# Chunks of 448 and 512 tokens, and tiles placed at chosen distances mod 256 bytes, in a spectral mixer with a squared-ReLU MLP

## The chip, the cores and the metric

The kernel runs on one core of a Trainium2 chip, in fp32 data with fp32r products. The metric is the device time of one execution in microseconds. The time before is 2588.85 us, the median of three runs (2587.41 to 2589.65).

## The reference

Eight sequences of 3008 tokens and 256 features go through a real FFT along the tokens, a complex 256 x 256 product with bias, a soft threshold and the inverse FFT, and then through an MLP of width 2048 whose activation is the square of a ReLU:

```python
X = np.fft.rfft(x, axis=1)
Yr = Xr @ w_r - Xi @ w_i + b_r
Yi = Xr @ w_i + Xi @ w_r + b_i
Yr = np.sign(Yr) * np.maximum(np.abs(Yr) - lam, 0.0)      # Yi alike
y = np.fft.irfft(Yr + 1j * Yi, n=3008, axis=1)
h = np.maximum(y @ w_in, 0.0)                             # 24064 tokens, 256 -> 2048
out = h * h @ w_out                                       # 2048 -> 256
```

## The kernel before

**Stages.** The transform of length 3008 is split as 47 x 64. For each sequence there are four kinds of small products: `psa` (length 47 forward, L867 and in the start phase L460), `psb` (length 64 forward, L320), `psm` (the complex 256 x 256 product, through `mix`), `psc` (length 64 back) and `psd` (length 47 back, L368). Their result lands, five columns of the 64 at a time ("units" of 235 tokens), in the tiles `xt0` and `xt1`: a high part and a low part of the MLP's input.

**The MLP** runs over chunks of tokens (`WIDTHS`, six per sequence: 470, four of 508, 506) and, within a chunk, over eight steps `j` of 256 hidden features. One pass (`j` of a chunk) is a round; there are 48 chunks and 384 rounds. A round has:

- `mm1`: twelve matmuls into `ph`, moving operand `xt` (one column per token of the chunk), stationary operand `wi`;
- `squares` (ACT, L1060 and L1061) into `g`, seven slots of half a chunk each; `sums` (DVE, L1069 to L1071) makes three of the seven slots by subtraction;
- a round later the split of `g` into `gh` (ACT, L1114) and `gl` (DVE, L1123);
- two rounds later `mm2`: twenty-one matmuls into `po`, moving operand `gh` or `gl` (one slot, half a chunk wide), stationary operand `wo`. The seven slots are the seven products of a Strassen step over (half of the tokens, half of the features), put together by `put_together` at the chunk's end.

Each product is made of three fp32r matmuls, high x high, high x low and low x high, by the helper `mm3` (L283; its three matmuls are L286, L287 and L288, whatever the product). Each matmul loads its 128 x 128 stationary operand anew.

**Order.** The main loop is written by hand (`manual_schedule`): `plan_a`, `plan_b` and `plan_d` put the steps of the next sequence's transform at places of a round (`load`, `a1`, `p1`, `v1`, `p2`, `a2`, `v2`), so `psm`, `psc`, `psa`, `psb` and `psd` stand between the `ph` and the `po` of a round or behind the `po`. `pieces` tells which chunks a unit lies in; a unit that lies across a border is written in two pieces. The start phase (about the first 122 us: the first sequence's transform and the splitting of the weights) has an order made by a small planner, `Queue`.

**Where tiles lie.** SBUF tiles are placed one behind the other in the order in which they are allocated, so each size moves all that follow. A distance below is the start of the stationary operand minus the start of the moving one, mod 256 bytes, as the tiles' sizes and this order give it:

| product | columns | moving operand starts at | stationary at | distance |
|---|---|---|---|---|
| `ph` | 470 to 508 | `xt` 112 to 224 | `wi` 96 | 128 to 240, in steps of 16 |
| `po` | 236, 254 | `gh`, `gl`: each slot 1016 bytes behind the last | `wo` 96 | 64 to 208, in steps of 8 |
| `psm`, main loop | 256 | `wm` 224 | `xh`, `xl` 160 | 192 |
| `psm`, start phase (L545, L550) | 512 | `wm` 224 | `xh`, `xl` 224 | 0 |
| `psc`, main loop | 512 | `zh` 32, `zl` 160 | `tMs` 128 | 96, 224 |

Of the kernel before, what the change touches and what calls it, by code (L numbers as in the profile page):

```python
# [28 lines left out]
F32 = mybir.dt.float32  # L29
F32R = mybir.dt.float32r  # L30
# [4 lines left out]
P = 128  # L35
S = 3008
N1 = 47
N2 = 64
NR = 24
# [5 lines left out]
W = 5  # L45
GROUPS = [(g, min(W, N2 - g)) for g in range(0, N2, W)]

NU1 = 96
# [11 lines left out]

WIDTHS = (2 * W * N1, 508, 508, 508, 508, 506)
NCH = len(WIDTHS)

# [182 lines left out]
def fft_mix_moe(ctx: ExitStack, tc: tile.TileContext, xp, xu, w_r, w_i, b_r, b_i,  # L246
# [7 lines left out]

    NCOL = max(WIDTHS)
    HALF = (NCOL // 2 + 1) // 2 * 2

# [5 lines left out]
    def ctile(name, shape, dt=F32):  # L263
        return const.tile(shape, dt, name=name, tag=name)

    tQ = ctile("tQ", [P, 64])
    tB = ctile("tB", [P, NR + 1, N2])
    tMs = ctile("tMs", [P, 2, P], F32R)
    tD = ctile("tD", [120, 4, 120])
    sg = ctile("sg", [P, 2, NR])  # L270
    neg = ctile("neg", [P, 1])
    nc.vector.memset(neg, -LAM)
# [63 lines left out]

    nch = NCH * B
    cols = [WIDTHS[c % NCH] for c in range(nch)]
    col0 = [sum(cols[:c]) for c in range(nch)]
    assert sum(WIDTHS) == S  # L340

# [36 lines left out]
    def start():  # L378

        with ExitStack() as own:  # L380
# [4 lines left out]
            def tl(tag, shape=(P, 512), dt=F32, bufs=1, name=None):  # L385
                return sb.tile(list(shape), dt, tag=tag, name=name or tag, bufs=bufs)
# [8 lines left out]
            tM = tl("tM", (P, P))  # L395
            tU = tl("tU", (NU1, 4 * NR))
            rows = tl("rows", (33, 2 * D), F32R)
# [64 lines left out]

            a_first, a_second, a0_done = [], [], []
            for i in range(nq):
                s = {}
# [310 lines left out]

            queue.run()
            return xt, later

# [8 lines left out]
    def tl(tag, shape=(P, 512), dt=F32, bufs=1, name=None):  # L788
        return sb.tile(list(shape), dt, tag=tag, name=name or tag, bufs=bufs)
# [4 lines left out]
    def opnd(name, dt):  # L794
        return tl(name, (P, NPR, HALF), dt, bufs=2)


# [88 lines left out]
    def plan_b(b, r0):  # L886
        for i in range(NPAIR):
            def steps(i=i):
# [16 lines left out]
                def high():  # L905
                    s["h"] = tl("xh", (P, 3, 2, P), F32R)
                    nc.scalar.copy(s["h"], s["x"])

                def low():
                    s["l"] = tl("xl", (P, 3, 2, P), F32R)  # L910
                    nc.vector.tensor_sub(s["l"], s["x"], s["h"].bitcast(F32))  # L911
# [64 lines left out]
    def plan_d(b, i, r, tag):  # L976
# [10 lines left out]
        def take():  # L987
            s["v"] = tl("xh", (P, 3, 2, P), name="dv").rearrange("p a b m -> p (a b m)")
            s["v"] = s["v"][:, :2 * NR * W].rearrange("p (k m) -> p k m", k=2)
            nc.scalar.copy(s["v"][:, :, :s["ps"].shape[3]], s["ps"][:, :, 1])  # L990

        def unfolded():
            if len(parts) == 1:
                x = tl("xl", (P, 3, 2, P), name="dx").rearrange("p a b m -> p (a b m)")
            else:
                x = tl("o0", (P, 2, HALF), name="dx").rearrange("p a m -> p (a m)")
            s["x"] = x[:, :2 * N1 * W].rearrange("p (k m) -> p k m", k=2)
            unfold(i, s["ps"], s["v"], s["x"])
# [74 lines left out]
    def mm2(c, j, po, gg):  # L1073
        m, _ = halves(cols[c])
        for s, bank, half in PLACES:

            mm3(po[bank][:, half * m:half * m + m], (wo_[0][j][:, s], wo_[1][j][:, s]),
                (gg[0][:, SLOT[s], :m], gg[1][:, SLOT[s], :m]), j == 0 and half == 0, j == NU - 1,
                skip_group_check=True)

    def put_together(c, po):
        n = cols[c]
        m, t0 = halves(n)
        p = {s: po[bank][:, half * m:half * m + m] for s, bank, half in PLACES}
        o = [tl(f"o{k}", (P, 2, HALF))[:, :, :m] for k in range(2)]
# [91 lines left out]
```

## Time and profile before

| | |
|---|---|
| time, median of three runs | 2588.85 us |
| span of the profiled execution | 2588.1 us |
| TensorE (PE) busy | 2562.5 us, 99% of the span |
| weight loads (PEld) busy | 2276.4 us, 88% |
| VectorE (DVE) busy | 2104.4 us, 81% |
| ScalarE (ACT) busy | 1990.3 us, 77% |
| mean granted TensorE clock | 0.997 |

The profiled execution's span runs from its first to its last instruction and lies 0.75 us below the median of the timed runs. In a timeline a row's first number is its start and the second its length; matmuls are pipelined, so a record's end lies behind the next one's start, and the distance of two starts is what a matmul costs.

### The profile page before, as it was taken

The page shows a single profiled execution, that of the slowest core. Times are in us where ns is not written, and L with a number is a line of the kernel's source. Part 1 is how long each engine was busy: PE and PEld are TensorE (multiplying, and loading weights), DVE is VectorE, ACT ScalarE, POOL GpSimd, SP SyncE. Part 2 cuts the span into 40 slices and gives each one's busy share as a digit, 9 for nine tenths or more (in the row PEclk, how much of TensorE's full clock was granted, in tenths as well). Part 3 has the DMA queues.
Part 4 walks back from the last instruction along what each step waited for, and adds up shares of the span by engine and source line. Part 5 has one row for each costly group of instructions (what it writes and reads, how often), then busy time and mean ns, then how long its engine had stood idle before and what let it go on. Part 6 is the DMA issues. An engine that isn't in the chain of part 4 may idle for free.

```text
span 2588.1 us, 43011 instructions
## 1 busy us (share of the span) xinstructions
PE 2562.5 (99%) x16674; PEld 2276.4 (88%) x16674; DVE 2104.4 (81%) x3441; ACT 1990.3 (77%) x3048; POOL 0.2 (0%) x4
## 2 busy tenths in 40 slices
PE   7999999999999999999999999999999999999999
PEld 4599988999889998899988999899998999999998
DVE  6888887888878888788887888788887888877777
ACT  4787886787777787788877878778886788787776
POOL 0000000000000000000000000000000000000000
PEclk8999999999999999999999999999999999999999
DMA  7711114111231112311132111321114111101000
GB/s 239 226 58 41 45 55 138 46 46 48 69 121 33 49 41 90 100 40 41 47 114 79 36 41 51 123 61 36 57 42 128 49 47 55 32 25 35 17 31 17
DMA packets 125362, 171.36 MB, mean 66 GB/s; under 512 B 13157, under 2 KB 88751, under 8 KB 125159
## 3 DMA queue, kind: packets, MB, share of 16 engines
q1 hardware_dynamic: 123851, 166.73, 20.7%
q8 instruction: 133, 2.18, 0.3%
q10 hardware_dynamic: 1308, 1.87, 0.2%
q14 instruction: 70, 0.57, 0.1%
HBM read 93.50 MB, written 74.97 MB: 65 GB/s over the span
## 4 chain that ended last, share of the span: by engine, by line
PE 96%; DVE 1%; DMA 1%; ACT 1%; SPq 0%; issue 0%; ACTq 0%; DVEq 0%
PE ph L286 13%; PE ph L288 13%; PE ph L287 13%; PE po L286 12%; PE po L287 12%; PE po L288 12%; PE psd L368 3%; PE psb L320 3%; PE psm L288 2%; PE psm L287 2%; PE psm L286 2%; PE psa L867 2%; PE psa L460 1%; PE psc L287 1%; PE psc L286 1%; PE psc L288 1%
## 5 line engine op out<-in xcount | busy, mean ns | idle before, releaser
L1114 ACT CAST gh<-g 128x762 fp32r<-128x762 f32 (+3 forms) x768 | 682.5, 927 | 325.0 <-PE po L288 284.6
L1123 DVE TENSOR_TENSOR gl<-g,gh 128x762 fp32r<-128x762 f32 (+3 forms) x768 | 805.6, 1070 | 107.5 <-ACT gh L1114 106.5
L286 PE MATMUL po<-gh,wo 128*128 128x254 f32 (+1 forms) x2688 | 765.1, 285 | 0.0
L287 PE MATMUL po<-gl,wo 128*128 128x254 f32 (+1 forms) x2688 | 753.3, 280 | 0.4 <-DVE gl L1123 0.4
L288 PE MATMUL po<-gh,wo 128*128 128x254 f32 (+1 forms) x2688 | 752.6, 280 | 0.0
L286 PE MATMUL ph<-xt,wi 128*128 128x508 f32 (+2 forms) x1536 | 608.7, 396 | 4.7 <-ACT g L1060 3.2
L288 PE MATMUL ph<-xt,wi 128*128 128x508 f32 (+2 forms) x1536 | 597.3, 389 | 0.0
L287 PE MATMUL ph<-xt,wi 128*128 128x508 f32 (+2 forms) x1536 | 596.2, 388 | 0.0
L286 PEld LDWEIGHTS po<-gh,wo 128*128 128x128 f32 x2688 | 509.6, 190 | 35.8 <-issue 29.2
L1060 ACT ACTIVATE g<-ph 128x508 f32<-128x508 f32 (+1 forms) x768 | 410.8, 587 | 153.2 <-PE ph L288 150.1
L287 PEld LDWEIGHTS po<-gl,wo 128*128 128x128 f32 x2688 | 509.5, 190 | 6.9 <-DVE gl L1123 0.6
L288 PEld LDWEIGHTS po<-gh,wo 128*128 128x128 f32 x2688 | 509.6, 190 | 0.0
L1069 DVE TENSOR_TENSOR g<-g 128x508 f32<-128x508 f32 (+1 forms) x384 | 261.4, 681 | 275.1 <-ACT g L1061 275.1
L1061 ACT ACTIVATE g<-g 128x1016 f32<-128x1016 f32 (+1 forms) x384 | 401.3, 1045 | 12.2
L288 PEld LDWEIGHTS ph<-xt,wi 128*128 128x128 f32 x1536 | 288.7, 188 | 62.3
L286 PEld LDWEIGHTS ph<-xt,wi 128*128 128x128 f32 x1536 | 289.5, 188 | 60.2 <-issue 9.7
L287 PEld LDWEIGHTS ph<-xt,wi 128*128 128x128 f32 x1536 | 289.3, 188 | 45.2
L1070 DVE TENSOR_TENSOR g<-g 128x254 f32<-128x254 f32 (+1 forms) x384 | 161.7, 421 | 13.2
L1071 DVE TENSOR_TENSOR g<-g 128x254 f32<-128x254 f32 (+1 forms) x384 | 161.5, 421 | 13.2
L288 PE MATMUL psm<-wm,xl 128*128 128x256 f32 x504 | 140.2, 278 | 0.3 <-DVE xl L911 0.3
L287 PE MATMUL psm<-wm,xh 128*128 128x256 f32 x504 | 140.2, 278 | 0.0
L286 PE MATMUL psm<-wm,xh 128*128 128x256 f32 x504 | 140.1, 278 | 0.0
(106 smaller groups left out, 2463.8 us busy)
## 6 DMA issues: line engine op xcount, KB each, us to landing
bin<-s SPq DMA_DIRECT2D x96, 256.0 KB
s<-evc SPq DMA_DIRECT2D x96, 256.0 KB
xin<-in_xp_dram SPq DMA_DIRECT2D x48, 512.0 KB
din<-s SPq DMA_DIRECT2D x94, 240.0 KB
s<-eva SPq DMA_DIRECT2D x208, 96.0 KB
outT_dram<-o SPq DMA_DIRECT2D x143, 127.0 KB
w<-in_moe_w_in_dram SPq DMA_DIRECT2D x8, 512.0 KB
w<-in_moe_w_out_dram SPq DMA_DIRECT2D x8, 512.0 KB
```

The lines of the kernel that those rows point to most:

```text
L286: nc.tensor.matmul(out, l0, r0, start=start, stop=False, **kw)
L287: nc.tensor.matmul(out, l0, r1, start=False, stop=False, **kw)
L288: nc.tensor.matmul(out, l1, r0, start=False, stop=stop, **kw)
L320: nc.tensor.matmul(ps[:, k, :, q, :], tv[:, q, k], tB[:, 0:r + 2:r + 1], start=True, stop=True)
L368: nc.tensor.matmul(ps[:, k, part], t[:n, s:s + P], tD[:n, tab + part, :n], start=True, stop=True)
L1060: nc.scalar.activation(g[:, a:b + 1:b - a, :m], ph[:, :, t * t0:t * t0 + m], AF.Relu)
L1061: nc.scalar.activation(g[:, LATER - 1:, :m], g[:, LATER - 1:, :m], AF.Square)
L1069: nc.vector.tensor_sub(g[:, :2, :m], at[1][:, None].broadcast_to([P, 2, m]), ends)
L1070: nc.vector.tensor_sub(at[6], at[3], at[4])
L1071: nc.vector.tensor_sub(at[1], at[6], at[2])
L1114: nc.scalar.copy(gg[k][0][:, part, :m], hid[k][:, part, :m])
L1123: nc.vector.tensor_sub(gg[k][1][:, part, :m], hid[k][:, part, :m], gg[k][0][:, part, :m].bitcast(F32))
```

## The change

1. The chunk widths become 470, four of 512 and 490 in the first sequence and 448 and five of 512 in the other seven (`FIRST`, `OTHER`).
2. `HALF`, the room of a half chunk in `g`, `gh`, `gl` and the output tiles, is 256 columns (before 254), so slots are 1024 bytes apart; the two halves of a PSUM bank in `po` are 256 columns apart whatever the chunk's width.
3. Tiles are placed anew: some are swapped or made larger, two unused ones (`pad0`, `pad1`) are put in between, and `xh` and `xl` of the main loop lie 64 bytes into a larger tile (`shifted`).

The distances become:

| product | columns | moving operand starts at | stationary at | distance |
|---|---|---|---|---|
| `ph` | 448 to 512 | `xt` 0 | `wi` 0 | 0 |
| `po` | 224 to 256 | `gh`, `gl` 0, each slot | `wo` 64 | 64 |
| `psm`, main loop | 256 | `wm` 0 | `xh`, `xl` 64 | 64 |
| `psm`, start phase | 512 | `wm` 0 | `xh`, `xl` 0 | 0 |
| `psc`, main loop | 512 | `zh`, `zl` 0 | `tMs` 0 | 0 |

```diff
-WIDTHS = (2 * W * N1, 508, 508, 508, 508, 506)
-NCH = len(WIDTHS)
+LINE = 16
+FIRST = (2 * W * N1, 512, 512, 512, 512, 490)
+OTHER = (448, 512, 512, 512, 512, 512)
+NCH = len(OTHER)
...
-    NCOL = max(WIDTHS)
-    HALF = (NCOL // 2 + 1) // 2 * 2
+    NCOL = max(FIRST + OTHER)
+    HALF = NCOL // 2
...
+    tD = ctile("tD", [120, 4, 120])
     tMs = ctile("tMs", [P, 2, P], F32R)
-    tD = ctile("tD", [120, 4, 120])
...
-    neg = ctile("neg", [P, 1])
+    neg = ctile("neg", [P, LINE])[:, :1]
...
-    cols = [WIDTHS[c % NCH] for c in range(nch)]
+    cols = [*FIRST] + [*OTHER] * (B - 1)
...
-            tU = tl("tU", (NU1, 4 * NR))
+            tU = tl("tU", (NU1, P))[:, :4 * NR]
...
+            ctile("pad0", [P, LINE])
...
+            ctile("pad1", [P, 3 * LINE])
...
+    def shifted(tag, dt=F32, name=None):
+        t = tl(tag, (P, 6 * P + 4 * LINE), dt, name=name)
+        return t[:, LINE:LINE + 6 * P].rearrange("p (a b m) -> p a b m", a=3, b=2)
...
-                    s["h"] = tl("xh", (P, 3, 2, P), F32R)
+                    s["h"] = shifted("xh", F32R)
...
-                    s["l"] = tl("xl", (P, 3, 2, P), F32R)
+                    s["l"] = shifted("xl", F32R)
...
-            mm3(po[bank][:, half * m:half * m + m], (wo_[0][j][:, s], wo_[1][j][:, s]),
+            mm3(po[bank][:, half * HALF:half * HALF + m], (wo_[0][j][:, s], wo_[1][j][:, s]),
...
-        p = {s: po[bank][:, half * m:half * m + m] for s, bank, half in PLACES}
+        p = {s: po[bank][:, half * HALF:half * HALF + m] for s, bank, half in PLACES}
```

On TensorE the order of the kinds of products stays as it was in every one of the 384 rounds. This is the first round of the second sequence's first chunk, from the last `ph` to the first `po` (which still belongs to the chunk before). In the kernel before:

```order
L286 MATMUL ph<-xt_4288,wi_276 128x470
L287 MATMUL ph<-xt_4289,wi_276 128x470
L288 MATMUL ph<-xt_4288,wi_277 128x470
L867 MATMUL psa<-xin,tQ 64x512 x4
L286 MATMUL po_4051<-gh,wo_1092 128x254
L287 MATMUL po_4051<-gl,wo_1092 128x254
L288 MATMUL po_4051<-gh,wo_1093 128x254
```

And in the changed one, whose last chunk of the first sequence has halves of 246 columns:

```order
L288 MATMUL ph<-xt_4290,wi_277 128x448
L289 MATMUL ph<-xt_4291,wi_277 128x448
L290 MATMUL ph<-xt_4290,wi_278 128x448
L875 MATMUL psa<-xin,tQ 64x512 x4
L288 MATMUL po_4053<-gh,wo_1094 128x246
L289 MATMUL po_4053<-gl,wo_1094 128x246
L290 MATMUL po_4053<-gh,wo_1095 128x246
```

The rows stand in the same places; the widths are others, and lines lie two further down.

On ACT the pieces of units change with the borders. Here is the second unit of the second sequence, written into `xt` from `dx`, before:

```order
L990 COPY dv<-psd 128x240
L1114 CAST gh<-g 128x762
L1114 CAST gh<-g 128x1016
L1003 CAST xt_4288<-dx 128x2x235
L1060 ACTIVATE g<-ph 128x508
```

In the changed kernel the border at 448 tokens cuts this unit into 213 and 22:

```order
L998 COPY dv<-psd 128x240
L1122 CAST gh<-g 128x3x246
L1122 CAST gh<-g 128x4x246
L1011 CAST xt_4290<-dx 128x2x213
L1068 ACTIVATE g<-ph 128x2x246 x2
L1069 ACTIVATE g<-g 128x4x246
L880 COPY eva<-psa 128x512
L1122 CAST gh<-g 128x3x246
L1122 CAST gh<-g 128x4x246
L1011 CAST xt_4420<-dx 128x2x22
```

One cast more stands there, a round later, and its subtraction on DVE likewise; this comes in seven of the eight sequences.

## Rows read from the trace of the kernel before

**Rows 1.** The page: span, busy time of the engines, chain that ended last.
```profile
span 2588.1 us, 43011 instructions
PE 2562.5 (99%) x16674; PEld 2276.4 (88%) x16674; DVE 2104.4 (81%) x3441; ACT 1990.3 (77%) x3048; POOL 0.2 (0%) x4
PE 96%; DVE 1%; DMA 1%; ACT 1%; SPq 0%; issue 0%; ACTq 0%; DVEq 0%
```

**Rows 2.** Waits of PE: who for whom, us in total, times, longest.
```profile
PE psb L320 <- DMA bin<-s: 7.5, 1, 7.5
PE psa L460 <- DMA x<-in_xu_dram: 4.0, 1, 4.0
PE ph L286 <- ACT g L1060: 3.2, 2, 1.7
...
PE po L287 <- DVE gl L1123: 0.4, 1, 0.4
```

**Rows 3.** Busy time of each engine in two stretches: 470-token chunk, 508-token chunk.
```profile
core 0: us, PE busy (x) PEld busy (x) DVE busy (x) ACT busy (x) POOL busy (x), PEclk, DMA share, GB/s
449.60:499.20 49.60, 49.60 (x348) 46.58 (x347) 41.59 (x72) 39.43 (x62) 0.00 (x0) 1.00 0.12 37
499.20:551.50 52.30, 52.30 (x352) 48.04 (x351) 44.85 (x73) 41.01 (x64) 0.00 (x0) 1.00 0.14 45
```

**Rows 4.** Timeline of PE, one round: start us, length us, line, instruction.
```profile
539.38 0.40 PE L286 MATMUL ph<-xt,wi 128*128 128x508 f32 x1
...
542.14 0.28 PE L286 MATMUL psm<-wm,xh 128*128 128x256 f32 x1
...
544.27 0.28 PE L286 MATMUL po<-gh,wo 128*128 128x254 f32 x1
...
546.75 0.39 PE L286 MATMUL ph<-xt,wi 128*128 128x508 f32 x1
```

**Rows 5.** Timeline of PE, one round of a 470-token chunk.
```profile
468.40 0.38 PE L286 MATMUL ph<-xt,wi 128*128 128x470 f32 x1
...
470.96 1.05 PE L368 MATMUL psd<-tD,din 120*128 120x120 f32 x8
471.77 0.36 PE L286 MATMUL po<-gh,wo 128*128 128x236 f32 x1
471.96 0.27 PE L287 MATMUL po<-gl,wo 128*128 128x236 f32 x1
...
474.20 0.28 PE L320 MATMUL psb<-tB,bin 128*128 128x128 f32 x1
```

**Rows 6.** Timeline of PE: the psm group of an earlier round.
```profile
501.59 0.28 PE L286 MATMUL psm<-wm,xh 128*128 128x256 f32 x1
...
503.63 0.28 PE L286 MATMUL po<-gh,wo 128*128 128x254 f32 x1
```

**Rows 7.** Groups by line: psm from 501.5, psm from 542.1; whole span.
```profile
L286 PE MATMUL psm<-wm,xh 128*128 128x256 f32 x6 | 1.7, 276 | 0.0
...
L286 PE MATMUL psm<-wm,xh 128*128 128x256 f32 x6 | 1.7, 280 | 0.0
...
L287 PE MATMUL psm<-wm,xh 128*128 128x256 f32 x504 | 140.2, 278 | 0.0
L287 PE MATMUL po<-gl,wo 128*128 128x254 f32 x2240 | 630.2, 281 | 0.4 <-DVE gl L1123 0.4
```

**Rows 8.** Timeline of PE in the start phase: psm at distance 0, 512 columns.
```profile
72.14 2.11 PE L545 MATMUL psm<-wm,xh 128*128 128x512 f32 x8
74.09 1.08 PE L550 MATMUL psm<-wm,xl 128*128 128x512 f32 x4
75.00 0.59 PE L575 MATMUL psc<-zh,tM 128*128 128x512 f32 x1
```

More of the change, by code (lines that the diff above doesn't have):

```diff
@@ L337, in fft_mix_moe @@
     nch = NCH * B
-    cols = [WIDTHS[c % NCH] for c in range(nch)]
+    cols = [*FIRST] + [*OTHER] * (B - 1)
     col0 = [sum(cols[:c]) for c in range(nch)]
-    assert sum(WIDTHS) == S
+    assert sum(FIRST) == sum(OTHER) == S
     def pieces(b, i):
@@ L987, in take @@
         def take():
-            s["v"] = tl("xh", (P, 3, 2, P), name="dv").rearrange("p a b m -> p (a b m)")
+            s["v"] = shifted("xh", name="dv").rearrange("p a b m -> p (a b m)")
             s["v"] = s["v"][:, :2 * NR * W].rearrange("p (k m) -> p k m", k=2)
@@ L993, in unfolded @@
             if len(parts) == 1:
-                x = tl("xl", (P, 3, 2, P), name="dx").rearrange("p a b m -> p (a b m)")
+                x = shifted("xl", name="dx").rearrange("p a b m -> p (a b m)")
             else:
```

## The prediction

> **What bounds the kernel now.** I read the page first: its busy shares, then the chain that ended last. TensorE is busy 99% of the span, and the chain is 96% PE [rows 1]. The waits of TensorE confirm it: the longest are single events of the start, 7.5 and 4.0 us, and inside the main loop the two that name ACT and DVE are worth 3.2 and 0.4 us in all [rows 2]. So in the main loop the end is set by the sum of distances between the starts of successive matmuls, which I call their pace, and by nothing else. The other engines have room: in two stretches of one chunk each DVE is busy 41.6 us of 49.6 and 44.9 us of 52.3, ACT less [rows 3].
>
> A pace is read from the timeline, not from the "mean ns" of a group: matmuls overlap, and a record lasts about 160 ns longer than its pace. One round of 508-token work shows it: twelve ph matmuls start at 539.38 and the next kind at 542.14, so 2.76 / 12 = 0.230 us each; eighteen psm of 256 columns take 544.27 - 542.14 = 2.13 us, 0.1183 each; twenty-one po of 254 columns take 546.75 - 544.27 = 2.48 us, 0.1181 each [rows 4]. A narrow round gives 470 columns in (470.96 - 468.40) / 12 = 0.2133 and 236 columns in (474.20 - 471.96) / 20 = 0.112 [rows 5]. Between the widths one column costs (0.230 - 0.2133) / 38 = 0.00044 us in ph and (0.1181 - 0.112) / 18 = 0.00034 us in po.
>
> **What the pace depends on.** The same psm group, same shapes and same addresses, takes 2.04 us for eighteen in another round (503.63 - 501.59), 0.1133 each [rows 6]. So there are two beats, 0.1133 and 0.1183, and a group keeps the beat that it began with: the mean record is 276 ns in the one group and 280 ns in the other on the lines of all its matmuls, and 278 over all 504 of a line [rows 6, 7], so about half the groups run in each. TensorE does not stream at a rate fixed by columns alone. The trace holds one kind of product whose two operands lie at a distance of 0 mod 256 in 512 columns: psm of the start phase (wm and xh at 224 both). Of one group the first eight take 74.09 - 72.14 = 1.95 us, some 0.10 of it, by my estimate, the switch from the kind before (in a narrow round the first po after another kind costs 471.96 - 471.77 = 0.19 against 0.112 [rows 5]), so (1.95 - 0.10) / 8 = 0.231 each; the last four take 75.00 - 74.09 = 0.91, 0.2275 each [rows 8]. It began slow and ended fast, where ph at distances of 128 to 240 stays at 0.230 for 508 columns, 0.2317 at 512.
>
> The Trainium skill says otherwise: on "SBUF — State Buffer", section "SBUF: two separate sides", PE, ACT and the dedicated ports of DVE never wait on anyone, and TensorE is given two independent read ports there. By it no address distance could matter, and the sum below would keep only its width terms. The two beats of one instruction form speak against it here, whatever their cause.
>
> **The change, part by part.** Nothing is removed and no matmul is added: 4608 ph and 8064 po matmuls before and after, in the same order of kinds in each of the 384 rounds.
>
> *Widths at unchanged paces.* Before, ph is 3072 of 508, 768 of 506 and 768 of 470: 3072 x 0.230 + 768 x 0.2291 + 768 x 0.2133 = 1046.3 us. After, it is 39 chunks of 512 (3744), 672 of 448, 96 each of 490 and 470: 3744 x 0.2317 + 672 x 0.2036 + 96 x (0.2221 + 0.2133) = 1046.1. po before: 6720 x 0.1181 + 1344 x 0.112 = 944.2. After: 6552 of 256 at 0.1188, 1176 of 224, 168 each of 246 and 236. Nothing here shows a po narrower than 236; going on by columns gives 0.1079, and no gain at all gives 0.112. I take 0.110, since each matmul still waits for a load of 128 columns of weights that gets no shorter. 778.4 + 129.4 + 168 x (0.1154 + 0.112) = 946.0. The widths alone therefore cost +1.6 us (between -1 and +4).
>
> *ph at distance 0.* Bounds for 512 columns: 0.2275, the end of the start-phase group, and 0.231, its beginning. A round has twelve ph in a row after another kind, as the group has twelve. I take 0.2285, nearer to the settled end, since from the second operand pair on every neighbour lies at the same distance and the group of the trace ended there: 0.0032 less than 0.2317, and the same for the narrow ones: 4608 x 0.0032 = 14.7 us gained (3 to 19).
>
> *po at distance 64.* Before, the distance changes with every slot (64 to 208, in steps of 8). After, all 21 of a round and the psm ahead of them have one distance, 64. The nearest row is psm at 256 columns: its distance is 192, that is 64 the other way round. Bounds are its two beats, 0.1133 and 0.1183, against 0.1188 at unchanged pace. I take 0.115, a third of the way up from the fast beat, since a group that once falls into a beat stays in it and a round now has 21 or 39 matmuls in which to fall in. 6552 x 0.0038 = 24.9 us gained (3 to 36). For the 1512 narrow ones I count nothing.
>
> *psm, psc, and the fp32 kinds.* psm goes from 192 to 64 and keeps two possible beats: nothing, within 3 us either way (1512 x 0.002). psc has 252 matmuls: under 1 us. The fp32 ones move with their tiles and have no change of form: nothing.
>
> *DVE and ACT.* Two columns more in 39 chunks and one more narrow chunk (its tiles become strided in rows of 224) in the place of wider ones; seven of the eight batches get one more unit that lies across a chunk border, so one ACT cast and one DVE subtraction more each. The cover is the room of both engines, 8 us per chunk on DVE [rows 3]; were it gone, an extra pair would cost under 1 us in each of seven batches.
>
> *PSUM halves 256 columns apart* and the pads change no instruction; nothing.
>
> Sum: +1.6 - 14.7 - 24.9 = -38.0 us. The profiled execution's span is 2588.1 us, 0.75 below the median of the three runs, so the sum goes against the median: 2588.85 - 38 = 2551.
>
> **Rivals.**
> *All settle.* ph at 0.2275 and po at 0.1133 everywhere: +1.6 - 4608 x 0.0042 - 6552 x 0.0055 = -53.8, 2535 us. For it: psm keeps 0.1133 through eighteen matmuls once there. Against it: half of the psm groups never get there.
>
> *Distance is worth nothing.* The beats come from something other than the operands' addresses (what ran ahead, or the state in which a group starts), and the new distances change only which rounds are lucky. Then the widths are left: 2588.85 + 1.6 = 2590 us, within what can be told from no change. For it: psm has both beats at one and the same distance. This is also the time by the rule of the Trainium skill told above.
>
> *One distance locks the slow beat.* Here is the case on the other side. With varying distances a bad neighbour costs one matmul; with one distance for all, a bad beat is kept through the group, as in the slow psm rounds. po would run at 0.1183 (6552 x 0.0005 = 3.3 gained). ph has no settled slow row at 512, so I double the gap of the two psm beats for the double width: 0.2275 + 0.010 = 0.2375, 4608 x 0.0058 = 26.7 lost. Together +1.6 - 3.3 + 26.7 = +25: 2614 us. It decides from a ph pace of 0.232 at 512 columns on (0.2317 and the 1.7 us that po and widths leave). For it: the first eight of the start group ran at 0.231. Against: they left it within the group.
>
> *Gain eaten by another engine.* If DVE or ACT ended the rounds, the gain would stop short. In the busier stretch of rows 3, TensorE would have to fall from 52.3 to 44.9 us before DVE's sum alone reaches it, and the forecast takes 1.5%. I give it no chance of its own.
>
> **How the numbers follow.** Forecast, partial settling (2540 to 2578): 0.52. All settle (2528 to 2540): 0.23. Nothing (2584 to 2594): 0.14. Slow lock (above 2594): 0.11. The likeliest gives 2551. For eight in ten, the range leaves out the slow lock and the faster edge of full settling and reaches to the case of nothing: 2531 to 2592. Differences under 0.2% (5 us) can't be told from no change in this kernel. Faster by more takes the first two cases and a little of what lies between: 0.78; same 0.12; slower 0.10.
>
> **What would show it.** In the profile after: the order of kinds unchanged, PE still the chain. In a steady round twelve ph of 512 columns should start within 2.74 us, and repeat 0.227 towards their end; twenty-one po of 256 within 2.42 us, many rounds at 0.1133; po of 224 near 0.110. The mean record of po should fall from 281 [rows 7] to about 277 while its columns rise by two. I am wrong if po's rounds show 0.118 or more, if ph of 512 stands at 0.232 or above, or if PE begins to wait for gh, gl or g.

## The result and the profile after

The changed kernel takes 2566.15 us (2564.71 to 2568.3, four runs) beside 2588.78 us (2587.41 to 2589.65) of the kernel before: a ratio of 0.9915, with a 95% interval of 0.9901 to 0.9929. That is 22.6 us less, where 38 were forecast. The range of 2531 to 2592 holds it.

The page of the profiled execution after, as [rows 1] of before (its run took 2566.42 us):

```profile
span 2564.6 us, 43025 instructions
PE 2538.0 (99%) x16674; PEld 2265.1 (88%) x16674; DVE 2102.8 (82%) x3448; ACT 1988.5 (78%) x3055; POOL 0.2 (0%) x4
PE 96%; DMA 1%; DVE 1%; ACT 1%; issue 0%; SPq 0%; ACTq 0%; DVEq 0%
```

Nothing has changed about the bound: TensorE is busy 99% of the span with the same 16674 matmuls, and the chain is PE. The waits of TensorE that answer to [rows 2] (who for whom, us in total, times, longest):

```profile
PE ph L288 <- ACT g L1068: 3.3, 2, 1.7
...
PE po L289 <- DVE gl L1131: 0.5, 1, 0.5
```

And two stretches, five rounds with a 448-column `ph` and seven with 512, with the columns of [rows 3]: DVE has 4.6 and 8.0 us to spare, and PE is never idle.

```profile
445.13:474.66 29.53, 29.53 (x217) 28.62 (x216) 24.89 (x47) 22.84 (x38) 0.00 (x0) 1.00 0.22 62
487.37:533.74 46.37, 46.37 (x311) 42.57 (x310) 38.38 (x64) 38.71 (x62) 0.00 (x0) 1.00 0.14 44
```

So the whole difference is pace. Timeline of TensorE after (start us, length us, line, instruction): a narrow round's `po`, a round with `psm`, and a `po` group that follows `psa`.

```profile
472.32 0.27 PE L288 MATMUL po<-gh,wo 128*128 128x224 f32 x1
...
474.66 0.37 PE L288 MATMUL ph<-xt,wi 128*128 128x448 f32 x1
...
513.49 0.40 PE L288 MATMUL ph<-xt,wi 128*128 128x512 f32 x1
...
515.33 0.39 PE L290 MATMUL ph<-xt,wi 128*128 128x512 f32 x1
...
516.23 0.28 PE L288 MATMUL psm<-wm,xh 128*128 128x256 f32 x1
...
518.35 0.28 PE L288 MATMUL po<-gh,wo 128*128 128x256 f32 x1
...
520.83 0.40 PE L288 MATMUL ph<-xt,wi 128*128 128x512 f32 x1
...
697.00 1.09 PE L875 MATMUL psa<-xin,tQ 47*64 47x512 f32 x8
698.02 0.38 PE L288 MATMUL po<-gh,wo 128*128 128x256 f32 x1
...
698.82 0.28 PE L288 MATMUL po<-gh,wo 128*128 128x256 f32 x1
...
700.52 0.40 PE L288 MATMUL ph<-xt,wi 128*128 128x512 f32 x1
```

Read against [rows 4, 5]: twelve `ph` of 512 columns take 516.23 - 513.49 = 2.74 us, 0.2283 each, against 0.230 for 508 before; the first eight take 1.84 us and the last four 0.90, 0.225 each as rounding allows (the starts of all groups give 0.2267). Eighteen `psm` take 2.12 us (0.1178), and twenty-one `po` of 256 columns 2.48 us (0.1181). Both sit in a slow beat. The third group shows that they need not: after `psa`, from the seventh matmul on, fifteen `po` take 700.52 - 698.82 = 1.70 us, 0.1133 each, with the same instruction and the same distance of 64. The narrow `po` of 224 columns takes 2.34 / 21 = 0.1114, no less than 236 columns did.

The groups by line, with the columns of [rows 7]:

```profile
L289 PE MATMUL po<-gl,wo 128*128 128x256 f32 x2184 | 612.3, 280 | 0.5 <-DVE gl L1131 0.5
...
L289 PE MATMUL psm<-wm,xh 128*128 128x256 f32 x504 | 141.2, 280 | 0.0
...
L289 PE MATMUL po<-gl,wo 128*128 128x224 f32 x392 | 107.6, 274 | 0.0
```

The mean record of `po` fell from 281 to 280 ns (277 was foretold), and that of `psm` rose from 278 to 280: more of its groups are slow than before.

To see where the time went, I added up, for each profiled execution, the distance from each start on TensorE to the next, by the kind of the matmul, over the main loop (from the first `ph` on). The waits are part of it, but as shown they are worth little. A sum comes from one execution: those of e2, e7 and e9 lie 2 to 3 us above the median of their kernel, and the start phase ahead of the sums lasts between 118.3 and 122.7 us, so two times can differ by a few us more or less than their sums do. All kernels of this text that do the whole work stand in one table; the times are medians. Each was timed beside the kernel before, whose median was 2587.3 to 2589.3 us.

| kernel | ph at | po at | sum ph | sum po | sum psm | sum psc | time |
|---|---|---|---|---|---|---|---|
| before | 128 to 240 | 64 to 208 | 1062.9 | 961.7 | 176.0 | 58.7 | 2588.78 |
| after | 0 | 64 | 1051.2 | 951.1 | 178.0 | 57.2 | 2566.15 |
| e1, old widths | 0 | 64 | 1056.3 | 958.7 | 176.7 | 58.6 | 2578.33 |
| e2, widths alone | 0 | 0 | 1055.0 | 966.6 | 181.3 | 58.8 | 2590.33 |
| e3 | 0 | 0 | 1051.6 | 967.2 | 178.2 | 57.3 | 2582.64 |
| e4 | 96 | 64 | 1067.8 | 939.4 | 178.9 | 58.8 | 2573.39 |
| e5 | 0 | 208 | 1048.7 | 957.7 | 178.0 | 57.2 | 2570.14 |
| e6 | 192 | 64 | 1051.5 | 933.0 | 175.7 | 58.3 | 2547.59 |
| e7 | 192 | 192 | 1052.3 | 937.9 | 176.0 | 58.3 | 2551.71 |
| e8 | 64 | 64 | 1065.2 | 933.7 | 174.7 | 58.7 | 2560.0 |
| e9 | 128 | 64 | 1064.6 | 933.0 | 176.0 | 58.7 | 2561.41 |

From before to after: ph -11.7, po -10.6, psm +2.0, psc -1.5, all else -1.7: -23.5 us, the difference of the two spans. The 1.7 us lie in the start phase: the first `ph` starts at 120.3 us in place of 122.1. Against the forecast (ph -0.2 - 14.7 = -14.9, po +1.8 - 24.9 = -23.1), `ph` came out nearly as foretold, and `po` brought under half.

### The profile page after: what moved, and what is told of

The parts are those of the page before. It is cut to its first block, busy times and chain, and to the rows that moved or that the text cites. A ratio compares the mean times of both kernels' runs of the same rounds, so it can differ in the third digit from the quotient of the medians.

```text
span 2564.6 us, 43025 instructions
## 1 busy us (share of the span) xinstructions
PE 2538.0 (99%) x16674; PEld 2265.1 (88%) x16674; DVE 2102.8 (82%) x3448; ACT 1988.5 (78%) x3055; POOL 0.2 (0%) x4
## 4 chain that ended last, share of the span: by engine, by line
PE 96%; DMA 1%; DVE 1%; ACT 1%; issue 0%; SPq 0%; ACTq 0%; DVEq 0%
PE ph L288 13%; PE ph L289 13%; PE ph L290 13%; PE po L288 12%; PE po L290 12%; PE po L289 12%; PE psd L370 3%; PE psb L322 3%; PE psm L290 2%; PE psm L288 2%; PE psm L289 2%; PE psa L875 2%; PE psm L548 1%; PE psc L289 1%; PE psc L288 1%; PE psc L290 1%
## 5 line engine op out<-in xcount | busy, mean ns | idle before, releaser
L1122 ACT CAST gh<-g 128x768 fp32r<-128x768 f32 (+6 forms) x768 | 682.8, 927 | 319.8 <-PE po L290 278.0
L1131 DVE TENSOR_TENSOR gl<-g,gh 128x768 fp32r<-128x768 f32 (+6 forms) x768 | 804.9, 1068 | 104.1 <-ACT gh L1122 104.0
L288 PE MATMUL po<-gh,wo 128*128 128x256 f32 (+3 forms) x2688 | 762.6, 284 | 0.0
L289 PE MATMUL po<-gl,wo 128*128 128x256 f32 (+3 forms) x2688 | 750.9, 279 | 0.5 <-DVE gl L1131 0.5
L290 PE MATMUL po<-gh,wo 128*128 128x256 f32 (+3 forms) x2688 | 750.8, 279 | 0.0
L288 PE MATMUL ph<-xt,wi 128*128 128x512 f32 (+3 forms) x1536 | 604.8, 394 | 4.7 <-ACT g L1068 3.3
L289 PE MATMUL ph<-xt,wi 128*128 128x512 f32 (+3 forms) x1536 | 594.4, 387 | 0.0
L290 PE MATMUL ph<-xt,wi 128*128 128x512 f32 (+3 forms) x1536 | 592.5, 386 | 0.0
L1068 ACT ACTIVATE g<-ph 128x512 f32<-128x512 f32 (+3 forms) x768 | 410.2, 587 | 138.2 <-PE ph L290 136.0
L1077 DVE TENSOR_TENSOR g<-g 128x512 f32<-128x512 f32 (+3 forms) x384 | 261.1, 680 | 261.4 <-ACT g L1069 260.4
L1069 ACT ACTIVATE g<-g 128x1024 f32<-128x1024 f32 (+3 forms) x384 | 400.8, 1044 | 12.2
L290 PEld LDWEIGHTS ph<-xt,wi 128*128 128x128 f32 x1536 | 288.5, 188 | 57.2
L1079 DVE TENSOR_TENSOR g<-g 128x256 f32<-128x256 f32 (+3 forms) x384 | 161.2, 420 | 13.2
L1078 DVE TENSOR_TENSOR g<-g 128x256 f32<-128x256 f32 (+3 forms) x384 | 161.1, 420 | 13.1
```

Of the source, the lines that this page charges most:

```text
L288: nc.tensor.matmul(out, l0, r0, start=start, stop=False, **kw)
L289: nc.tensor.matmul(out, l0, r1, start=False, stop=False, **kw)
L290: nc.tensor.matmul(out, l1, r0, start=False, stop=stop, **kw)
L1068: nc.scalar.activation(g[:, a:b + 1:b - a, :m], ph[:, :, t * t0:t * t0 + m], AF.Relu)
L1069: nc.scalar.activation(g[:, LATER - 1:, :m], g[:, LATER - 1:, :m], AF.Square)
L1077: nc.vector.tensor_sub(g[:, :2, :m], at[1][:, None].broadcast_to([P, 2, m]), ends)
```

## Experiments

The first theory was the prediction's: each kind of product pays a price for its own distance, and a long row at one distance falls into the fast beat. The rivals: distance is worth nothing and the widths do it; or the beat hangs on the state in which a group is entered.

### One kind at a time, over all distances (p1)

A kernel that has only groups of one kind of product: 21 matmuls of 256 columns or 12 of 512, two stationary and two moving operands in the order of `mm3`, at 16 distances, each group entered from one plain fp32 matmul of 64, 66 or 68 columns.

```diff
+    for n, count, entries in NS:
+        for start in (0, 8):
+            for d in range(0, 64, 4):
+                for e in range(entries):
+                    gap(64 + 2 * e)
+                    group(f"n{n}s{4 * start}d{4 * d}x", n, count, start, start + d)
```

> A kernel of its own that leaves the whole computation out (its output is zeros): TensorE alone runs groups of fp32r matmuls in the pattern of mm3, 21 of 256 columns and 12 of 512, at every distance from 0 to 240 bytes in steps of 16 between the stationary and the moving operand, each with the moving operand at 0 and at 32 mod 256, and each entered after fp32 matmuls of two or three different lengths. Theory 'distance': at 256 columns the groups differ by distance, between 113.3 and 118.3 ns per matmul; at 64 with the moving operand at 0 most entries give 117.7 and few 113.3, as in the changed kernel; at 512 columns distance 0 ends at 226.7 and others lie up to 236. Rival 'nothing in the distance': every distance gives the same pace within 1 ns, and what differs goes by the entry alone.

Settled pace in ns (mean of the spacings from the sixth on) at ten of the sixteen distances; two numbers where groups at the same distance differ:

| distance | 0 | 32 | 64 | 96 | 128 | 160 | 192 | 208 | 224 | 240 |
|---|---|---|---|---|---|---|---|---|---|---|
| 256 columns | 120 | 118 | 117.8 or 113.3 | 117.7 or 120 | 118.7 | 120 | 117.8 | 116.5 or 120 | 116.7 or 117.8 | 116.7 or 120 |
| 512 columns | 230.8 or 226.7 | 233.3 | 233.3 | 234.6 | 232.4 | 233.4 | 228.8 | 231.6 | 233.2 | 228.6 or 226.7 |

Timeline rows of TensorE in it (a row here is a whole group; its length is that of all its matmuls; the name gives columns, start and distance):

```profile
19.62 2.76 PE L285 MATMUL n256s0d0x<-moving,still 128*128 128x256 f32 x21
...
52.19 2.72 PE L285 MATMUL n256s0d64x<-moving,still 128*128 128x256 f32 x21
54.89 2.65 PE L285 MATMUL n256s0d64x<-moving,still 128*128 128x256 f32 x21
...
279.70 3.01 PE L285 MATMUL n512s0d0x<-moving,still 128*128 128x512 f32 x12
282.69 2.99 PE L285 MATMUL n512s0d0x<-moving,still 128*128 128x512 f32 x12
...
315.82 3.05 PE L285 MATMUL n512s0d96x<-moving,still 128*128 128x512 f32 x12
```

Distance does set the pace: with nothing else changed, 512 columns run between 226.7 and 234.8 ns and 256 between 113.3 and 120.3 (118.3 was expected as the upper end). At 0 only two of the four groups of 512 columns end at 226.7, and one group at 144, a distance that is not in the table, does so too. Where both operands start mod 256 matters less: moved by 32 bytes together, most distances kept their pace. But at 64, the distance of `po`, the same group took 2.72 us or 2.65, and all that differed is what ran ahead of it (two of the six groups at 64 are fast).

### The widths or the distances (e1, e2, e3)

e1 is the changed kernel with the old chunk widths; slots and halves stay 256 columns apart.

```diff
-FIRST = (2 * W * N1, 512, 512, 512, 512, 490)
-OTHER = (448, 512, 512, 512, 512, 512)
+FIRST = OTHER = (2 * W * N1, 508, 508, 508, 508, 506)
...
-    NCOL = max(FIRST + OTHER)
+    NCOL = 512
```

> The changed kernel with the chunk widths of the kernel before (470, four of 508, 506), slots still 256 columns apart and all tiles where the change puts them: distances 0, 64, 64 and 0 with the old widths. If the gain of 22.6 us comes from the distances: 2566 within 5 us, ph of 508 columns near 0.227. If it comes from the widths: 2589 within 4 us. If settling needs operands of whole 64-byte lines (512 and 256 columns, not 508 and 254): in between, 2575 to 2585.

Measured: 2578.33 us, a ratio of 0.9961 (0.9947 to 0.9974), so 12 us of the 22.6 are lost with the widths. The widths were forecast to cost 1.6. The time lies in the third case's range, but for another reason than the one given there: `ph` of 508 columns does settle (0.2282 in the mean of the spacings behind the first), and it is `po` that reaches neither beat of 64: all 317 groups of 254 columns settle at 0.1183.

e2 is the kernel before with the new widths and the slots and halves 256 columns apart, and with nothing placed.

```diff
-WIDTHS = (2 * W * N1, 508, 508, 508, 508, 506)
+FIRST = (2 * W * N1, 512, 512, 512, 512, 490)
+OTHER = (448, 512, 512, 512, 512, 512)
...
-    HALF = (NCOL // 2 + 1) // 2 * 2
+    HALF = NCOL // 2
```

> The kernel before with the new widths, the slots and PSUM halves 256 columns apart, and none of the pads, swaps or shifts: rows of 512 and slots of 256 columns make all distances of ph, po and psm 0, with moving operands at 224 mod 256. If ph gains by distance 0, ph of 512 columns at 0.229 as in the changed kernel. If po needs its 64: po of 256 columns at 0.119 or above, against 0.1172, and 2575 to 2582 in all. If 64 is worth nothing to po: 2566 within 4 us. If the start of the operands mod 64 decides (224 is 32 mod 64) ph will not settle: 2585 or more.

Measured: 2590.33 us, 1.0007 (0.9998 to 1.0016). So without the placement the widths bring nothing. They do not leave the distances alone: with slots of 1024 bytes every distance of `ph`, `po` and `psm` becomes 0, `ph` gains 7.9 us, and `po` and `psm` lose 4.9 and 5.3. `ph` at 0.2292 and `po` at 0.1198 are as expected for distances of 0; the time is 8 us above the 2582 that went with them, and the loss in `psm` had not been counted. Widths and placement can't be priced apart: in e1 `po` of 254 columns has the sum 958.7, 7.6 above the changed kernel, at the same distance and with fewer columns.

e3 is the changed kernel without the two pads, so that `wo` too starts at 0 mod 256.

```diff
-            ctile("pad0", [P, LINE])
...
-            ctile("pad1", [P, 3 * LINE])
```

> The changed kernel without the two unused pads: po's stationary operand at 0 as the moving one, so distance 0 for po, all else as in the changed kernel. If 64 is what po gains by: po of 256 columns at 0.119 or above and 2578 within 5 us. If the distance of po is worth nothing: 2566 within 3 us. If 0 is better for po than 64 (it settles at 512 columns): po at 0.114 to 0.115, 2548 to 2555.

Measured: 2582.64 us, 0.9977 (0.9967 to 0.9986). Two unused tiles of 64 and 192 bytes are worth 16 us, all of it `po` (967.2 against 951.1; its groups settle at 0.1198, near p1's 0.120 at distance 0). The pair of kernels differs mod 256 in one operand's address alone. This takes down the rival that distance is worth nothing. The Trainium skill, page "SBUF — State Buffer", section "SBUF: two separate sides", says that PE never waits on anyone and has two independent read ports. That speaks of engines in each other's way; that no distance between PE's own two operands could matter was the prediction's inference from it, and these 16 us refute the inference.

### The price of ph's distance (e4), and another distance for po (e5)

e4 puts `ph` at 96, the slowest distance of p1, and leaves `po` and `psm` at 64: a third unused tile ahead moves `wi`, and a larger `pad0` puts the rest back.

```diff
+            ctile("pad2", [P, 24])
...
-            ctile("pad0", [P, LINE])
+            ctile("pad0", [P, 56])
```

> The changed kernel with wi moved by 96 bytes and wo kept at 64: ph's distance is 96 in place of 0, po and psm as in the changed kernel. Theory 'distance': ph of 512 columns at 234 in place of 229 ns, 4608 x 5 ns = 23 us more, 2589 within 5 us. Rival 'what ph gains comes from whole lines of 512 columns, not from its distance': 2566 within 4 us.

Measured: 2573.39 us, 0.9945 (0.9933 to 0.9957). `ph` does settle at 0.2340 and costs 16.6 us more than in the changed kernel. But the time rose by 7 only, where 23 was expected, since `po`, of which nothing was touched, gave back 11.7. Timeline of TensorE in e4, two rounds, the first with `psc` and the second with `psm` ahead of the `po`:

```profile
509.91 0.40 PE L288 MATMUL psc<-zh,tMs 128*128 128x512 f32 x1
...
510.61 0.28 PE L288 MATMUL po<-gh,wo 128*128 128x256 f32 x1
...
512.99 0.40 PE L288 MATMUL ph<-xt,wi 128*128 128x512 f32 x1
...
515.80 0.28 PE L288 MATMUL psm<-wm,xh 128*128 128x256 f32 x1
...
517.92 0.28 PE L288 MATMUL po<-gh,wo 128*128 128x256 f32 x1
...
520.40 0.39 PE L288 MATMUL ph<-xt,wi 128*128 128x512 f32 x1
```

Behind `psc` twenty-one `po` take 2.38 us (0.1133), behind `psm` 2.48 (0.1181). I sorted all `po` groups of 256 columns by the kind that runs ahead of them and counted those under 115 ns:

| ahead of po | after (ph at 0) | e4 (96) | e6 (192) | e8 (64) | e9 (128) | e7 (192, po at 192) |
|---|---|---|---|---|---|---|
| psa | 32 of 32 | 31 | 31 | 27 | 31 | 15 |
| psd | 8 of 80 | 80 | 71 | 61 | 68 | 0 |
| psm | 6 of 70 | 2 | 67 | 64 | 63 | 70 |
| psc | 0 of 76 | 75 | 60 | 76 | 68 | 75 |
| ph | 2 of 51 | 1 | 43 | 22 | 49 | 22 |
| all 309 | 48 | 189 | 272 | 250 | 279 | 182 |

It is not chance: of the 40 places (a round of a sequence and the kind ahead of its `po`) that come five times or more, at least 35 have the same beat every time in each of these kernels, and the others all but once. Nor is it the addresses of `po` itself: its PSUM tiles are the same in every round, and of the two buffers that `gh` and `gl` take in turns each has 16 fast groups of 16 behind `psa` after the change. Behind `psm` the rule is plain: in all five kernels with both at 64, each of the 70 `po` groups has the beat of the `psm` group ahead of it (after: 64 slow and 6 fast pairs, e4 68 and 2, e6 3 and 67, e8 6 and 64, e9 7 and 63).

e5 puts `po` at 208, where p1 had 0.1165 in five of six groups, by starting `gh` and `gl` 112 bytes further on.

```diff
+    def moved(name, by):
+        t = tl(name, (P, NPR * HALF + 4 * LINE), F32R, bufs=2)
+        return t[:, by:by + NPR * HALF].rearrange("p (a m) -> p a m", a=NPR)
...
-                gg[k] = opnd("gh", F32R), opnd("gl", F32R)
+                gg[k] = moved("gh", 28), moved("gl", 28)
```

> The changed kernel with gh and gl 112 bytes into larger tiles, so that po's distance is 208 in place of 64, all else as it was. Theory 'distance', by the first probe: po of 256 columns at 116.6 in place of 117.2 ns, 6552 x 0.6 = 4 us less, 2562 within 3 us. Rival 'po needs starts at whole 64-byte lines': po at 119 or above, 2578 or more.

Measured: 2570.14 us, 0.9933 (0.9919 to 0.9947), 4 above the changed kernel and neither the 2562 of the theory nor the 2578 of the rival. `po` settled at 0.1183, in all 309 groups between 0.1182 and 0.1186, a pace that p1 does not have at 208, and `ph`, of which nothing was touched, gained 2.5 us. So a price list of single kinds does not carry over into the loop; whether the start at 112 or the neighbours made the difference is open.

### Two kinds in turns (p2)

A second kernel that leaves the work out: four turns of twelve matmuls of 512 columns and twenty-one of 256, with the distance of one varied while that of the other stays at 0 (512) or 64 (256).

```diff
+    for d in range(0, 64, 2):
+        turn(f"o{4 * d}", 0, d, 0)
+    for d in range(0, 64, 2):
+        turn(f"h{4 * d}", d, 16, 0)
```

> A kernel of its own that leaves the whole computation out (its output is zeros): TensorE alone runs what a round has without the transform, twelve matmuls of 512 columns and then twenty-one of 256, four times over for each setting. First the distance of the 256-column ones goes from 0 to 248 in steps of 8 with 512 at 0, then that of the 512-column ones with 256 at 64, then the second moving operand alone is moved by 16 to 240 bytes. Theory 'distance': the four turns of a setting repeat each other from the second on, 512 columns are fastest at 0 or 240 (227 to 229 ns) and slowest near 96 (234), 256 columns fastest at 208 and 224 (116.6) and slowest at 0 and 112 (120). Rival 'the entry decides': the order of the settings in the first probe does not return, and turns of one setting differ from each other.

Timeline of TensorE, the second turn of two settings (the number behind h is the distance of the 512 columns; the 256 are at 64 in both):

```profile
702.09 2.91 PE L294 MATMUL h0hx<-moving,still 128*128 128x512 f32 x12
704.84 2.64 PE L300 MATMUL h0ox<-moving,still 128*128 128x256 f32 x21
707.31 2.91 PE L294 MATMUL h0hx<-moving,still 128*128 128x512 f32 x12
...
1209.38 2.91 PE L294 MATMUL h192hx<-moving,still 128*128 128x512 f32 x12
1212.13 2.55 PE L300 MATMUL h192ox<-moving,still 128*128 128x256 f32 x21
1214.52 2.91 PE L294 MATMUL h192hx<-moving,still 128*128 128x512 f32 x12
```

The 512 columns take 2.75 us in both, and the 256 columns 2.47 us behind distance 0 and 2.39 behind 192. The pair of the changed kernel costs 5.22 us a turn, the pair of 192 and 64 costs 5.14, the least of the 64 settings of both. With the 256 columns at 64, their beat changes with the neighbour's distance.

Three things here go beyond the pair. At 64 for both kinds the 256 columns are slow in every turn of this kernel, though fast in p3 and in e8 below. At some settings the turns differ from each other, as the rival had it; at 16 they are slow, fast, slow, fast. Here are the 256 columns of the first and the second turn there, each with the 512 that follow:

```profile
741.65 2.64 PE L300 MATMUL h16ox<-moving,still 128*128 128x256 f32 x21
744.12 2.96 PE L294 MATMUL h16hx<-moving,still 128*128 128x512 f32 x12
746.92 2.55 PE L300 MATMUL h16ox<-moving,still 128*128 128x256 f32 x21
749.31 2.96 PE L294 MATMUL h16hx<-moving,still 128*128 128x512 f32 x12
```

They take 2.47 and 2.39 us with the same operands (the PSUM tile is another one from turn to turn, which was not tried apart). And with 512 at 0 and 256 at 64, moving the second moving operand alone puts the 256 columns between 115.6 and 119.2 ns, so the distance of one pair of operands is not the whole address pattern. The kind's own distance counts as well: with 512 at 0 the 256 columns run from 113.3 ns (at 88, 5.15 us a turn) to 121.2 (at 24). 88 was not tried in the kernel.

This is the second theory: **the beat of a group is settled by how it is entered, so it hangs on its neighbours' distances as well as on its own.**

### The same in the kernel (e6), and in a copy of the loop's order (p3)

e6 is the changed kernel with `ph` at 192, all else as it is.

```diff
+            ctile("pad2", [P, 48])
...
-            ctile("pad0", [P, LINE])
+            ctile("pad0", [P, 32])
```

> The changed kernel with wi moved by 192 bytes and wo kept at 64: ph's distance 192, po's 64. In the second probe this pair took 5.140 us a turn against 5.220 for the changed kernel's pair (ph 229.4 in place of 228.5, po 113.5 in place of 117.8). If the state carried from ph to po decides, and psm, psc and psd in between do not spoil it: 384 x 0.08 = 31 us less than the changed kernel, 2536; spoilt in two of three rounds: 2556. Rival 'each distance has its price', by the first probe: ph 230 in place of 229 and po as it was, 4 us more, 2570.

Measured: 2547.59 us (2546.5 to 2548.36), 0.9844 (0.9831 to 0.9858). It is the fastest kernel of the study, 18.6 us below the changed one, where 31 were reckoned if all rounds gained and 10 if one in three did; the rival's 2570 is out. Its `ph` has the same sum as at 0 (1051.5), and `po` gained 18.1 us without a change of its own. The round that answers to the one of after:

```profile
512.17 0.39 PE L288 MATMUL ph<-xt,wi 128*128 128x512 f32 x1
...
514.92 0.28 PE L288 MATMUL psm<-wm,xh 128*128 128x256 f32 x1
...
516.97 0.28 PE L288 MATMUL po<-gh,wo 128*128 128x256 f32 x1
...
519.35 0.39 PE L288 MATMUL ph<-xt,wi 128*128 128x512 f32 x1
```

`ph` 2.75 us, `psm` 2.05 (2.12 after), `po` 2.38 (2.48 after). 272 of the 309 `po` groups are fast, and 80 of the 84 `psm` groups, where after had 19 and before 34. The waits of TensorE that name ACT and DVE are the same 3.3 and 0.5 us, but the chain is 94% PE here, with 2% each of ACT and DVE (96%, 1% and 1% after).

p3 leaves the work out too: it repeats a cycle of three rounds in the order of the main loop (ph, psm, po; ph, psd, po, psb; ph, psc, po) for 64 pairs of distances.

```diff
+    for dh in range(0, 64, 8):
+        for do in range(0, 64, 8):
+            cycle(f"h{4 * dh}o{4 * do}", dh, do)
```

> A kernel of its own that leaves the whole computation out (its output is zeros): TensorE alone runs the three rounds of the main loop over and over (ph, psm, po; ph, psd, po, psb; ph, psc, po) with psm at 64 and psc at 0, for every pair of distances of ph and po that is a multiple of 32. Theory 'the state at entry, carried from group to group': the sum of three rounds goes by the pair and not by adding a cost of ph's distance and one of po's; the pair 0 and 64 of the changed kernel gives po near 117.2, the pair 96 and 64 gives ph 234 with po near 115, as the fourth experiment did. Rival 'each distance has its price': ph's pace in a pair goes by its own distance alone and po's by its own, within 0.5 ns.

The cycle (third minus second) takes from 20.026 us (ph at 192, po at 192) to 20.573 (96, 160). By pair, for the third cycle: `ph` in the mean of its three rounds and `po` behind psm, psd and psc, in ns from start to start behind the first spacing:

| ph, po | cycle, us | ph | po | the kernel at this pair: po behind psm, psd, psc |
|---|---|---|---|---|
| 0, 64 | 20.267 | 229.4 | 117.8, 117.7, 117.8 | slow, slow, slow |
| 96, 64 | 20.266 | 233.9 | 117.8, 113.5, 113.3 | slow, fast, fast |
| 192, 64 | 20.293 | 229.8 | 117.8, 117.7, 117.8 | fast, fast, fast |
| 64, 64 | 20.087 | 233.3 | 113.3, 114.1, 113.5 | fast, fast, fast |
| 128, 64 | 20.074 | 233.0 | 113.3, 113.5, 113.3 | fast, fast, fast |
| 192, 192 | 20.026 | 229.1 | 113.3, 117.8, 113.4 | fast, slow, fast |

```profile
161.99 2.91 PE L293 MATMUL h0o64hx<-moving,still 128*128 128x512 f32 x12
166.86 2.64 PE L293 MATMUL h0o64ox<-moving,still 128*128 128x256 f32 x21
...
1142.67 2.96 PE L293 MATMUL h64o64hx<-moving,still 128*128 128x512 f32 x12
1147.51 2.54 PE L293 MATMUL h64o64ox<-moving,still 128*128 128x256 f32 x21
```

The last column is from the count above, by what most groups do. Five of the six pairs agree, to the kind of round; 192 and 64 does not. The rows show the pair of the changed kernel and that of e8: with `ph` 0.05 us slower per twelve, `po` is 0.10 faster per twenty-one. At 64 and 64 the first cycle still has the slow beat behind psm and psd, and the later two do not. Only at 64 and at 192 does `po` come to 113.3 in this kernel: at 0 and at 160 it stands near 120 in every third cycle, whatever the distance of `ph`.

### Three more pairs in the kernel (e7, e8, e9)

The edits are the sizes of the three pads `pad2`, `pad0` and `pad1` (in columns of 4 bytes; 0 is without): e7 48, 0, 16; e8 16, 0, 48; e9 32, 48, 48. In e8 the 64 bytes of `pad0` are moved ahead of `wi`, so by the order of the tiles `wi` alone lies elsewhere than in the changed kernel.

> The changed kernel with ph at a distance of 192 (64 bytes the other way than po's 64) and po at 192 as well; psm stays at 64, psc at 0. The pace is read as settled start-to-start time. Theory A (what a po group does is decided by how it is entered, so only a run of the same order of kinds tells it, and the probe with three kinds of rounds is such a run): there ph stood at 0.229, po at 0.1133 in two of three rounds and at 0.1178 in the third, psm at 0.1135. On the kernel, against the changed one: 6552 po x (0.1172 - 0.1148) = 15.7 us and 1512 psm x 0.0043 = 6.5 us gained, ph nothing: 2544 us, beside 2547.6 of ph at 192 and po at 64. Theory B (each kind has a price for its own distance, wherever it comes from): po of 256 columns at 192 was 0.1178 in the first probe, so po is no faster than in the changed kernel, and ph at 192 costs nothing: 2566 to 2570 us.

> The changed kernel with ph at a distance of 64 in the place of 0; po and psm at 64 as there. In the probe with three kinds of rounds ph stood at 0.2333 and po and psm at 0.1134. Theory A (ph pays its own distance and po gains by the way it is entered): 4608 x (0.2333 - 0.2290) = 20 us lost, 6552 x (0.1172 - 0.1135) = 24 gained, psm 6 gained: 2556 us, faster than the changed kernel although its ph is slower. Theory B (each kind has a price for its own distance): 20 us lost and nothing gained: 2586 us.

> The changed kernel with ph at a distance of 128; po and psm at 64. In the probe with three kinds of rounds ph stood at 0.2327, po and psm at 0.1134. Theory A: 4608 x (0.2327 - 0.2290) = 17 us lost, 24 gained on po, 6 on psm: 2553 us. Theory B: 17 lost and nothing gained, 2583 us.

Measured: e7 2551.71 us, 0.986 (0.9846 to 0.9875); e8 2560.0, 0.9892 (0.9877 to 0.9907); e9 2561.41, 0.9894 (0.9877 to 0.991). Theory A foretold 2544, 2556 and 2553, B 2566 to 2570, 2586 and 2583. All three are nearer to A, and e8 is the clear case: one tile moved by 64 bytes, a `ph` 14.0 us slower than in the changed kernel, and a kernel faster by 6 us, since `po`, whose addresses are the same, is faster by 17.4. A's sizes were too good by 4 to 8 us: `po` gained 17.4 in e8 where 24 were reckoned, and `psm` 3.3 where 6 were. Timeline of TensorE in e8, a round with `psm`:

```profile
510.82 0.39 PE L288 MATMUL ph<-xt,wi 128*128 128x512 f32 x1
...
513.62 0.28 PE L288 MATMUL psm<-wm,xh 128*128 128x256 f32 x1
...
515.66 0.28 PE L288 MATMUL po<-gh,wo 128*128 128x256 f32 x1
...
518.04 0.39 PE L288 MATMUL ph<-xt,wi 128*128 128x512 f32 x1
```

`ph` 2.80 us (2.74 after), `psm` 2.04, `po` 2.38.

e7 shows the entry best, with the rounds sorted as in p3. Timeline of TensorE in e7, `po` behind `psm` and, a round later, behind `psd`:

```profile
517.37 0.28 PE L288 MATMUL po<-gh,wo 128*128 128x256 f32 x1
...
519.75 0.39 PE L288 MATMUL ph<-xt,wi 128*128 128x512 f32 x1
...
522.50 1.05 PE L370 MATMUL psd<-tD,din 120*128 120x120 f32 x8
523.31 0.36 PE L288 MATMUL po<-gh,wo 128*128 128x256 f32 x1
...
525.87 1.05 PE L322 MATMUL psb<-tB,bin 128*128 128x128 f32 x8
```

Behind `psm` 2.38 us. Behind `psd` 2.56, of which some 0.08 belong to the switch of kinds (as in [rows 5]); the rest is the slow beat. At this pair 70 of 70 are fast behind `psm` and 0 of 80 behind `psd`.

## Why the prediction came out as it did

**The bound** was right. The order of kinds and the waits stayed, 21.8 of the 23.5 us between the two spans are the pace of the main loop, and no other engine took any of it. The other 1.7 us came in the start phase and were not taken apart.

**ph at distance 0** was right. 0.2285 was taken, and the groups stand at 0.2290 in the mean. They enter as the start-phase group of [rows 8] did: the medians of the first five spacings are 233, 236, 228, 233 and 231 ns, and from the sixth on 227. The sum fell by 11.7 us, where -14.9 was reckoned.

**po at distance 64** is the term that was mis-sized: 0.115 was taken, and it measured 0.1172, 6552 x 0.0022 = 14 us short. The round read above even shows 0.1181, which the prediction had named as a sign of being wrong. The step that failed is the reason given for going down to a third above the fast beat, that a group which falls into a beat stays there and that a round has 21 or 39 matmuls in which to fall in. The first half holds for both beats: 261 of the 309 groups stayed at 0.1177 to 0.1178 through all 21 matmuls, and 64 of the 70 behind `psm` are slow, each behind a slow `psm`. The slow beat is as stable as the fast one, and which it is comes from what ran ahead: 32 of 32 groups behind `psa` are fast, 0 of 76 behind `psc`, and in e8 a move of `ph`'s operand alone turned 0 of 76 into 76 of 76. The prediction had the evidence in its own rows: `psm` at one distance has both beats, each kept for eighteen matmuls [rows 4, 6]. I read it as how far a group gets, and it was how it is entered. That the time fell among those of partial settling is in part luck, for `po` did not settle in part: by an estimate from these paces, some 6.5 of its 10.6 us come from the slow beat lying below the 0.1188 of the mixed distances (6552 x 0.0010), and some 4.6 from the 48 of 309 groups that are wholly fast (48/309 x 6552 x 0.0045).

**The widths** were forecast at +1.6 us at unchanged paces. The 224 columns were taken at 0.110 and measured 0.1118: against 236 columns nothing is gained, and the bound 0.112 was the right end (1176 x 0.0018 = 2 us). Beyond that no run shows the term: with old widths in the new places (e1) the kernel loses 12 us, and with new widths and no placement (e2) the distances change too. That e2 came out 1.6 us above the kernel before, just as this term would have it, is a balance of gains and losses in `ph`, `po` and `psm`, and chance. Width and distance act together.

**psm and psc** were counted at nothing within 3 us and under 1: +2.0 and -1.5 us, so `psc` gained a little more than was allowed for. 19 of 84 `psm` groups are fast after, 34 before.

**The rivals.** "Distance is worth nothing" is refuted by e3 (16 us for one operand's place), yet the reason it gave, what ran ahead or the state in which a group starts, is half of the answer. "One distance locks the slow beat" is what happened to `po`, but its price was taken from the wrong kind: the slow beat at 64 is 0.1178 and still below the 0.1188 of the mixed distances, and `ph`, which was to pay 26.7 us, did not lock. "All settle" was not reached by any kernel here: e6 comes within 13 us of its 2535 with the same matmuls in the same order, and has 272 of 309 `po` groups fast.

**What stays open**: what the state is that a group hands on. p3 copies the order of kinds and still has the pair of 192 and 64 wrong, so something that it leaves out belongs to it; the places of the other tiles and the other kinds are candidates. That was not taken apart further.

## What to carry to other kernels

When TensorE is busy all the time and the waits are gone, measure the spacing of starts by kind and by what ran ahead: a group with two beats at the same addresses has time left, which its busy share of 99% does not show. Choose operand addresses by trying pairs in the kernel itself, since prices from one kind alone misled here (e5 lost where a gain was reckoned, and e8 has the slower `ph` and the lower time). Two or three unused tiles are a cheap knob: they moved this kernel between 2547.59 and 2582.64 us with not one instruction changed in form.

## What the runs showed of the hardware

- Start-to-start time of an fp32r matmul depends on the distance of its two operands mod 256 bytes: 113.3 to 120.3 ns for 256 columns and 226.7 to 234.8 for 512 in p1, at a granted clock of 1.0 (the 2.4 GHz level; 0.998 in the mean of the changed kernel). No settled group of p1 was faster than 113.3 and 226.7. The Trainium skill, page "TensorE: Matmul & The Clock Gate", section "Back-to-back issue gap", gives N / 2.4 + 2.5 ns at the full clock as the gap of an isolated matmul, and sets a stream of weight loads and matmuls apart from it; worked out from that formula as an estimate, 256 and 512 columns would take 109.2 and 215.8 ns, and no settled group here comes to it.
- At some distances a group has two stable beats, 113.3 and 117.8 ns at 64, and what ran ahead of it chooses one (p1, p3, e8, and the count by kinds above).
- 224 columns of `po` cost as much as 236: 111.8 and 111.9 ns in the changed kernel.
